# Two transformer layers on one core: q, k and v of three chunks computed with seven products for eight

## The chip, the cores and the metric

The kernel runs on one core of a Trainium2 chip. The metric is device time in microseconds (us), from the start of the program to its end. The core has a matrix engine (TensorE, PE in the profile; its weight loads are PEld), a vector engine (VectorE, DVE), a scalar engine (ScalarE, ACT), GpSimd (POOL), and SyncE (SP), which here only issues DMAs. Each engine works through its own queue in order. TensorE reads from the on-chip memory SBUF and accumulates into banks of PSUM.

## The reference

Two layers, each an attention block and an MLP block on `x` of 2048 tokens by 1024 features; both layers use the same weights.

```python
def _A_ref(x, wqkv, wo):                 # 32 heads of 32
    q, k, v = split(x @ wqkv)            # wqkv: 1024 x 3072
    # token t attends to t, t-2, ..., t-14 of its own head
    logits = einsum("bhsd,bhswd->bhsw", q, kg) * 32 ** -0.5   # masked where t-2w < 0
    o = einsum("bhsw,bhswd->bhsd", softmax(logits), vg)
    return o @ wo

def _B_ref(x, w1, w3, w2):               # w1, w3: 1024 x 3584, w2: 3584 x 1024
    return (silu(x @ w1) * (x @ w3)) @ w2

x = x + _A_ref(layernorm(x), wqkv, wo)
x = x + _B_ref(layernorm(x), w1, w3, w2)
x = x + _A_ref(layernorm(x), wqkv, wo)
x = x + _B_ref(layernorm(x), w1, w3, w2)
```

## The kernel before

**Chunks and units.** The tokens are cut into four chunks of 512 (`CH`); a unit `(l, c)` is the MLP of layer `l` on chunk `c`. The order of the program is: q, k, v of layer 0 for its four chunks (`first_q`, `q_part`), then for `u` from 0 to 7 the MLP of unit `u` (`b_stage`), and after units 1 to 4 the q, k, v of unit `u + 3`, that is of the four chunks of layer 1 (`with_q`). Attention runs in between on VectorE in halves of 256 tokens (`score_steps`, `value_steps`), its small gather and spread matmuls and the output projection (`o_tile`, L773) are put between matmuls of other work. Output projections of a chunk are done while the MLP of the chunk before it runs.

**Plain q, k, v.** `q_part` makes one of q, k, v for a chunk: for each of 8 column tiles, 8 matmuls of 128x128 by 128x512 into a PSUM bank (L831), whose stationary side is every eighth column of the weight tile (`t::KT`); ScalarE copies the bank to a stage tile (L835); two tiles at a time are stored to DRAM (`qkv_d`, L842), from where attention loads them. In layer 0 the stage tiles lie in `big`, in layer 1 in `hT`. Three parts make 192 matmuls a chunk.

**The Strassen form.** From unit 2 on (`TU`) the MLP's products use a form with 7 products for 8. `products` cuts the normalised chunk `xnT` into four quarters (two halves of features, two of 256 tokens); `norm_sums` (L288) makes three sums of quarters in `sums` and one in place; the weights come as blocks and sums of blocks that were written to DRAM earlier (`t_d`). A product is 8 matmuls of 128x128 by 128x256 (`run`, L1133). One group makes 512 output features: products P1, P5, P6, P2 use an `early` weight tile of 1 MB, P7, P3, P4 a `late` one of 768 KB. `head_part` also holds the steps between the products: ScalarE copies of accumulators (L1162, L1167, L1171), a VectorE addition (L1174), the corner on VectorE (L1186, L1189). Groups are chained: P7, P3, P4 of a group are put between P1, P5, P6 and P2 of the next. At the end of the chain `W("P1", ...)`, the first down projections, stand between the last group's tail. The down projection uses the same form (`second`, `W`, L1068).

**Sums of weights.** Units 0 and 1 run the plain form, and beside it `weight_size` squares each w1 or w3 tile on ScalarE (L871), a ones-matmul (L883) adds up, `scale_of` (L859 to L863, VectorE) makes a power-of-two scale; `weight_sums` (L901, ScalarE) casts four blocks to scaled fp16 in one of two slots in `big`, `differences` (L914, VectorE) makes three more, and two DMAs of POOL's queue write them to `t_d`. w2 is measured in layer 0's q, k, v (`part_of_w2`, L948) and summed in the down projections (L995).

**The planner.** The order of instructions is written out by the Python program, which keeps a planned clock of each engine (`now`). `pe`, `dve`, `act`, `dma` add costs to it. Work that isn't tied to a place lies in queues: `norms, makes, adds, values, scores` for VectorE (`background` takes what would end before a given time), `acts, sizes, parts, reads` for ScalarE (`act_background` takes what would end by TensorE's planned time plus 2.2 us), `pe_queue` for small matmuls. `force`, `finish_sums`, `ready_norm` emit what must be done at a point.

**Weights.** Six tiles of 1 MB (`wp`) are filled in the order of the list `seq`; `release(n)` lets n go and `flush` issues the next loads on SP's queue (L709 to L720). `held` and `release_held` keep tiles until their sums are made.

**Normalisation.** For the later chunks it runs on ScalarE (`act_norm`: L313 measures, L340 applies), and a DMA transpose on SP's queue (L342) puts it into one of two `xnT` buffers; for an MLP unit `norm_sums` follows. Side PSUM tiles (tag `sd`, two) hold projections, attention and the sums of sizes.

Of the kernel before, what the change touches and what calls it, by code (L numbers as in the profile page):

```python
# [17 lines left out]
def kernel(  # L18
# [13 lines left out]
    nc = tc.nc  # L32
# [122 lines left out]

    def bank(name):
        if name == "po":
            return side.tile([P, 512], FP32, name=name, tag="sd")
        return psum.tile([P, 512], FP32, name=name, tag="mm")
# [52 lines left out]
    up2 = const.tile([P, 1], FP32, name="up2")  # L212
    peak = const.tile([P, 3], FP32, name="peak")
    hsum = const.tile([P, HTN // 2, HT], FP16, name="hsum")
    h16 = hT[:].bitcast(FP16)
    t2_d = [dram.tile([P, 7, (b - a) // 2, 512], FP16, name=f"t2_d{i}") for i, (a, b) in enumerate(fsplits)]
    t_d = [[dram.tile([P, 14, KT // 2, P], FP16, name=f"t_d{m}_{g}") for g in range(NG)] for m in range(2)]
    qkv_d = [[dram.tile([P, KT, S], BF16, name=f"qkv_d{l}_{i}") for i in range(3)] for l in range(2)]
# [58 lines left out]
    def norm_sums(key):  # L277
# [9 lines left out]
        def step(out, x, y, op):  # L287
            return 0.62, xnT_at[key], lambda: nc.vector.tensor_tensor(out, x, y, op=op)  # L288
# [66 lines left out]

    def act_background():
        for queue in (acts, sizes, parts, reads):
            while True:
                s = head(queue)
                if s is None or max(now["act"], s[1]) + s[0] > now["pe"] + 2.2:  # L360
                    break
# [207 lines left out]
    def score_steps():  # L569

        V = nc.vector
        for g, (l, h) in enumerate(halves):
# [19 lines left out]
            def gather_heads(t):  # L592
                at["L"] = L = side.tile([P, W, BLK], FP32, name="L", tag="sd")
# [42 lines left out]
            def spread_heads(a, At=At, An=An, t2=t2, key=(l, h)):  # L636
                ps = side.tile([P, W, BLK], FP32, name="pe", tag="sd")
# [43 lines left out]
    for u in range(len(units)):  # L681
# [14 lines left out]
        if 1 <= u and u + 3 < len(units):  # L696
            seq += [("qkv", which, h) for which in range(3) for h in range(2)]
    w_tiles, w_at, due, used = [], {}, [], [0]
# [58 lines left out]
    def o_tile():  # L757
# [12 lines left out]
        for hh in range(2):  # L770
# [8 lines left out]
            dve(0.64, r)  # L779
# [12 lines left out]
    def between(hold, must=False):  # L792

        flush()
# [20 lines left out]
    def q_part(l, c, which, ws, then=()):  # L815
# [8 lines left out]
        for t0 in range(0, KT, SG):  # L824
            i = (c * 3 + which) * KT // SG + t0 // SG
            i = i % (7 if l == 0 else 8) * SG
            sgt = big[:, i * CH:(i + SG) * CH].bitcast(BF16).rearrange("p (a t) -> p a t", a=SG) if l == 0 else hT[:, i:i + SG, :]
# [16 lines left out]
            if l == 0:  # L844
                stored[:] = landed, landed
# [19 lines left out]
    def weight_size(m, g, w, at, got):  # L865
# [8 lines left out]
        def scale_item(ps, r):  # L874
            def emit():
                scale_of(ps[:], up, down)
                got["at"] = now["dve"] + 0.1
            yield 0.8, r, emit

        def add_up(t):  # L880
            ps = side.tile([P, 1], FP32, name="size", tag="sd")
            for i in range(2):
                nc.tensor.matmul(ps[:], lhsT=ones[:], rhs=size[:, m, g, i:i + 1], start=i == 0, stop=i == 1)  # L883
            makes.append([scale_item(ps, pe(2, t)), None])
# [4 lines left out]
    def weight_sums(m, g, w, got):  # L889
# [4 lines left out]
        for a in range(2):  # L894
# [9 lines left out]
            makes.append([differences(m, g, a, now["act"] + 0.1), None])  # L904
# [482 lines left out]
```

## Time and profile before

| | us |
|---|---|
| median of 3 runs | 1568.73 (1568.36 to 1570.1) |
| profiled execution | 1568.03 |
| its span | 1566.3 |
| TensorE busy / VectorE / ScalarE | 1543.1 / 1190.8 / 913.5 |
| q, k, v of layer 1 begin at | 536.5, 726.1, 917.0, 1104.9 |

The span is from the first to the last instruction; the execution holds 1.7 us around it. A line of the profile names the source line, the engine, the operation, what it writes and reads, shapes and count; then busy time, mean length of one, and the idle time just before it with what ended it. A matmul's length (379 ns for 512 columns) is its passage through the array; matmuls overlap, so their rate is read from starts.

### The profile page before, as it was taken

How to read it: one execution, taken by the hardware profiler on the slowest of the kernel's cores; microseconds unless marked ns; L12 is line 12 of the kernel's file. 1: busy time of each engine (PE TensorE's matmuls, PEld its weight loads, DVE VectorE, ACT ScalarE, POOL GpSimd, SP SyncE). 2: the span in 40 equal slices, each digit the busy share in tenths (PEclk: the TensorE clock that was granted, in tenths of full speed). 3: DMA queues.
4: the chain of work that ended last, by engine and by line, in shares of the span. 5: the costliest groups of instructions: out<-in, count | busy, mean ns of one | idle time of the engine just before them, and what ended most of it. 6: DMA issues, size and time to landing. Idle time of an engine off the chain costs nothing.

```text
span 1566.3 us, 25242 instructions
## 1 busy us (share of the span) xinstructions
PE 1543.1 (99%) x9758; PEld 999.6 (64%) x9758; DVE 1190.8 (76%) x2048; ACT 913.5 (58%) x1452; POOL 125.2 (8%) x247
## 2 busy tenths in 40 slices
PE   9999999999998999999999999999999999999999
PEld 7665544444443568585676857767677667676866
DVE  4789988988887798998779775897368977445345
ACT  4785466575755447565556754756648356544634
POOL 1111001110111100100002020000101000000000
PEclk9999999999999999999999999999999999999999
DMA  9666767898787987888869878797979977878885
GB/s 329 196 186 211 233 192 270 291 284 282 219 300 269 275 319 260 288 298 296 277 239 322 288 272 280 267 331 260 315 270 303 313 285 261 314 273 329 314 293 207
DMA packets 258360, 431.17 MB, mean 275 GB/s; under 512 B 72832, under 2 KB 200064, under 8 KB 241984
## 3 DMA queue, kind: packets, MB, share of 16 engines
q1 hardware_dynamic: 248464, 390.90, 74.9%
q0 software_dynamic: 9632, 38.54, 6.3%
q8 instruction: 76, 1.25, 0.3%
q14 instruction: 44, 0.36, 0.1%
q10 hardware_dynamic: 144, 0.13, 0.0%
HBM read 345.90 MB, written 67.90 MB: 264 GB/s over the span
## 4 chain that ended last, share of the span: by engine, by line
PE 77%; DVE 12%; DMA 6%; ACT 3%; issue 1%; SPq 0%; POOL 0%; ACTq 0%; DVEq 0%; POOLq 0%
PE st L1133 30%; PE ps L831 15%; PE w L1068 14%; PE po L773 6%; PE pg L1254 4%; PE pu L1263 4%; PE acc L1285 3%; DMA t_d<-big 2%; DVE tree L503 2%; DVE tree L583 2%; DVE tree L667 2%; DMA kT<-qkv_d 1%; DMA x_sb<-in_A_x_dram 1%; DVE st L233 1%; PE pe L638 1%
## 5 line engine op out<-in xcount | busy, mean ns | idle before, releaser
L831 PE MATMUL ps<-xnT,wqkv 128*128 128x512 f16 (+1 forms) x1472 | 322.2, 379 | 0.0
L1133 PEld LDWEIGHTS <-early 128*128 128x128 f16 x2688 | 262.7, 98 | 42.5 <-issue 2.7
L831 PEld LDWEIGHTS <-wqkv 128*128 128x128 bf16 x1472 | 210.8, 144 | 108.4 <-issue 1.7
L1068 PE MATMUL w<-t,hT 128*128 128x512 f16 x1008 | 226.3, 379 | 2.1 <-ACT big L1088 1.9
L1133 PEld LDWEIGHTS <-late 128*128 128x128 f16 x2016 | 196.8, 98 | 33.0 <-issue 3.8
L583 DVE TENSOR_TENSOR tree<-qT,kT 128x2048 bf16<-128x2048 bf16 x128 | 156.4, 1222 | 39.6 <-DMA kT<-qkv_d 22.8
L503 DVE TENSOR_TENSOR tree<-tree 128x1024 bf16<-128x1024 bf16 x256 | 175.4, 686 | 0.8
L1133 PE MATMUL st<-xnT,late 128*128 128x256 f16 x1344 | 174.2, 273 | 1.0 <-ACT big L1171 0.9
L1133 PE MATMUL st<-big,early 128*128 128x256 f16 x1344 | 172.4, 273 | 2.7 <-DVE big L288 1.3
L1068 PEld LDWEIGHTS <-hT 128*128 128x128 f16 x1008 | 98.3, 98 | 115.2 <-issue 3.4
L667 DVE TENSOR_TENSOR tree<-At,vT 128x2048 bf16<-128x2048 bf16 x128 | 156.3, 1221 | 14.2 <-ACT At L640 13.0
L1133 PE MATMUL st<-xnT,early 128*128 128x256 f16 x1344 | 166.0, 273 | 0.0
L773 PE MATMUL po<-wo,oT 128*128 128x512 bf16 x512 | 117.6, 382 | 7.3 <-DVE up_scale L859 2.9
L1162 ACT COPY st<-st 128x512 f32<-128x512 f32 x84 | 48.6, 579 | 116.7 <-PE st L1133 116.0
L1263 PE MATMUL pu<-xnT,w3t 128*128 128x512 f16 x448 | 105.8, 379 | 1.2 <-DMA w3t<-in_B_w_dram 0.7
L1254 PE MATMUL pg<-xnT,w1t 128*128 128x512 f16 x448 | 105.8, 379 | 0.0
L835 ACT CAST hT<-ps 128x512 bf16<-128x512 f32 x96 | 55.8, 586 | 82.0 <-PE ps L831 81.1
L1174 DVE TENSOR_TENSOR st<-st,big 128x512 f32<-128x512 f32 x84 | 58.5, 696 | 58.6 <-ACT big L1171 58.4
L1285 PE MATMUL acc<-w2t,hT 128*128 128x512 bf16 x448 | 98.2, 379 | 0.0
L1142 ACT ACTIVATE sg<-st,down_scale 128x512 bf16<-128x512 f32 x126 | 86.8, 689 | 12.7 <-PE st L1133 12.3
L773 PEld LDWEIGHTS <-oT 128*128 128x128 bf16 x512 | 50.5, 99 | 65.1 <-issue 10.4
L1133 PE MATMUL st<-big,late 128*128 128x256 f16 x672 | 87.1, 273 | 0.0
(171 smaller groups left out, 1946.4 us busy)
## 6 DMA issues: line engine op xcount, KB each, us to landing
early<-t_d SPq DMA_DIRECT2D x84, 1024.0 KB, 6.7
late<-t_d SPq DMA_DIRECT2D x84, 768.0 KB, 6.1
t<-t_d SPq DMA_DIRECT2D x42, 1024.0 KB, 6.6
t<-t_d SPq DMA_DIRECT2D x42, 768.0 KB, 5.1
wqkv<-in_A_wqkv_dram SPq DMA_DIRECT2D x28, 1024.0 KB, 8.5
w1t<-in_B_w_dram SPq DMA_DIRECT2D x14, 1024.0 KB, 8.0
w3t<-in_B_w_dram SPq DMA_DIRECT2D x14, 1024.0 KB, 9.2
t_d<-big POOLq DMA_DIRECT2D x28, 512.0 KB, 6.1
```

Source lines behind the costliest of these rows:

```text
L503: nc.vector.tensor_tensor(b, b, buf[:, 4:8, :], op=ALU.add)
L583: V.tensor_tensor(pr, qT[:], kT[:, :, k0:k0 + TCH], op=ALU.mult)
L667: V.tensor_tensor(tm, At[:], win, op=ALU.mult)
L773: nc.tensor.matmul(ps[:], lhsT=oT[:, t, j * P:(j + 1) * P], rhs=wo[:, t, hh * 512:(hh + 1) * 512], start=(t == 0), stop=(t == KT - 1))
L831: nc.tensor.matmul(ps[:], lhsT=ws[kk // KH][:, kk % KH, t::KT], rhs=xnT[:, kk, :], start=(kk == 0), stop=(kk == KT - 1))
L1068: nc.tensor.matmul(out[:], lhsT=lhs[:, k, j * P:(j + 1) * P], rhs=w[:, k, :], start=start and k == 0, stop=k == nq - 1, skip_group_check=True)
L1133: nc.tensor.matmul(out[:, a, :], lhsT=w[:, a, blk, k, :], rhs=rhs[:, k, :], start=start and a == 0 and k == 0, stop=k == KQ - 1, skip_grou ...
L1142: nc.scalar.activation(sg[:], src, ACTF.Silu, scale=inv)
L1174: nc.vector.tensor_tensor(G["D"][:], G["D"][:], su, op=ALU.add)
L1254: nc.tensor.matmul(pg[:], lhsT=w1t[:, kk, fi * P:(fi + 1) * P], rhs=xnT[:, kk, :], start=(kk == 0), stop=(kk == KT - 1))
L1263: nc.tensor.matmul(pu[:], lhsT=w3t[:, kk, fi * P:(fi + 1) * P], rhs=xnT[:, kk, :], start=(kk == 0), stop=(kk == KT - 1))
L1285: nc.tensor.matmul(acc[:], lhsT=hT[:, f, j * P:(j + 1) * P], rhs=tiles[hh][f // nq][:, f % nq, :], start=(f == 0), stop=(f == f1 - f0 - 1))
```

## The change

For the chunks 1, 2 and 3 of layer 1 `q_products` takes the place of `q_part`: six groups (q, k, v, each with two halves of 512 features) in the chained form, which `products` and `q_products` now share as `pipeline`. Chunk 0 of layer 1 and all of layer 0 stay plain. `t_d` gets entries 2 to 4 for wq, wk, wv, and `seq` their early and late tiles.

The sums of wqkv have one scale. ScalarE squares the six wqkv tiles in layer 0's first chunk (`size_of_qkv`). The sums for v are made from the third chunk on, in one block slot (4, in `hT`), those for q and k while chunk 0 of layer 1 runs, in slots 2, 3 and 4 (`sums_of_qkv`); for that chunk the stage tiles move to `hsum` and two rows of `hT`. Weight tiles of that chunk are let go through `held`, after their sums.

`sums`, the single buffer of token sums, is also used for the three chunks: `sum_later` is queued for them after their norm, and becomes free at the end of `q_products`.

Side tiles are now taken with `side_tile`, which first emits scale items that are open; scale items go to the head of `makes`. `act_background` has a gate of 5.0 us until the first chained stage, and 2.2 from there. Planned costs of VectorE steps and some of ScalarE are set anew. One of the differences of weights is computed from another, as an addition.

```diff
+    def side_tile(*args, **kw):
+        while opened[0]:
+            assert head(makes) is not None
+            take(makes)
+        return side.tile(*args, **kw)
...
+    room = [hT[:, 2:9, :].bitcast(FP16), hT[:, 9:16, :].bitcast(FP16)]
+    blocks += [big[:, 3072:6656].rearrange("p (b k c) -> p b k c", b=7, k=KT // 2)]
+    blocks += [r_.rearrange("p b (k c) -> p b k c", k=KT // 2) for r_ in room]
...
+    gate = [5.0]
...
-                if s is None or max(now["act"], s[1]) + s[0] > now["pe"] + 2.2:
+                if s is None or max(now["act"], s[1]) + s[0] > now["pe"] + gate[0]:
...
+        elif TU <= u and u + 3 < len(units):
+            groups = [(2 + which, g) for which in range(3) for g in range(2)]
+            for i, (m, g) in enumerate(groups):
+                seq += [("early", m, g)] + ([("late", *groups[i - 1])] if i else [])
+            seq += [("late", *groups[-1])]
...
+            if (l, c) == (1, 0):
+                i = (which * KT + t0) // SG % 3
+                sgt = (hsum_slots + [hT[:, 0:2, :]])[i]
...
-            makes.append([scale_item(ps, pe(2, t)), None])
+            makes.insert(0, [scale_item(ps, pe(2, t)), None])
...
+    def size_of_qkv(i, w):
+        ...
+            yield 1.95, 38.0, lambda: nc.scalar.activation(junk, w_[:, j * half:(j + 1) * half], ACTF.Square,
+                                                          accum_out=size_q[:, 2 * i + j:2 * i + j + 1])
...
+    def sums_of_qkv(which, ws):
+        while "at" not in got_q or norm_left.get(("Q", 0, NCH - 1), 1):
+            yield "blocked"
+        for g in range(2):
+            for a in range(2):
+                slot = 4 if which == 2 else (2, 3, 4, 2, 3, 4, 3, 4)[q_blocks[0]]
+                ...
+                    t = 4 * g + 2 * fh + a
+                    yield 0.61, max(got_q["at"], stored[slot]), lambda: nc.scalar.activation(
+                        b[:, i], ws[kh][:, :, t::KT], ACTF.Copy, scale=up_q[:])
+                makes.append([differences(2 + which, g, a, slot, now["act"] + 0.1), None])
...
+    def q_products(l, c):
+        key = ("Q", l, c)
+        ready_norm(key)
+        force(adds, lambda: key in sums_of)
+        ...
+        def consume(G, q, src, r):
+            pair, t0 = q % 2, HT * (q // 2)
+            to = stage(G, pair)
+            if q != 3:
+                nc.scalar.activation(to[:, :, t0:t0 + HT], src, ACTF.Copy, scale=down_q[:])
+            ...
+            if not G["left", pair]:
+                nc.sync.dma_start(qkv_d[l][which][:, t:t + SG, c * CH:(c + 1) * CH], to)
+        ...
+        pipeline(key, groups, consume, lambda i: between(False, i == 3))
+        sums_free[0] = True
+        xnT_free[key] = now["pe"]
...
             if f0 == 0 and i == 4 and 1 <= u and q < len(units):
                 queue_norm(("Q", *units[q]), units[q][1], range(R))
+                if u >= TU:
+                    adds.append([sum_later(("Q", *units[q])), None])
...
-        if with_q:
+        if with_q and u >= TU:
+            q_products(*units[q])
+        elif with_q:
             for which in range(3):
                 if which == 2:
                     between(False, True)
-                q_part(*units[q], which, [weight("qkv"), weight("qkv")])
-                release(2)
+                ws = [weight("qkv"), weight("qkv")]
+                if which < 2:
+                    reads.append([sums_of_qkv(which, ws), None])
+                q_part(*units[q], which, ws)
+                held.append(("q", which))
+                release_held(1)
+            finish_sums(lambda: q_blocks[0] > 6)
+            force(makes, lambda: not pending[2])
```

## The prediction

> **What bounds the kernel now.** I read the page's busy times first, then the matrix engine's timeline around one qkv stage of layer 1, the table of stretches, the groups by form and the DMA issues. Busy times, of a span of 1566.3 us:
>
> ```profile
> PE 1543.1 (99%) x9758; PEld 999.6 (64%) x9758; DVE 1190.8 (76%) x2048; ACT 913.5 (58%) x1452; POOL 125.2 (8%) x247
> ```
>
> TensorE is idle for 1566.3 - 1543.1 = 23.2 us only, so a gain must come from fewer or shorter matmuls, or from those 23 us. The timeline of TensorE (start, length, line, operation, count) shows the stage that the change rewrites, and the form that it is rewritten to:
>
> ```profile
> 917.01 41.60 PE L831 MATMUL ps<-xnT,wqkv 128*128 128x512 f16 x192
> 958.45 1.04 PE L1133 MATMUL st<-xnT,early 128*128 128x256 f16 x8
> ...
> 1001.73 1.04 PE L1133 MATMUL st<-xnT,early 128*128 128x256 f16 x8
> ...
> 1019.19 1.04 PE L1133 MATMUL st<-xnT,early 128*128 128x256 f16 x8
> ```
>
> 192 plain matmuls take 958.45 - 917.01 = 41.44 us, 215.8 ns each, without a gap. From 1001.73 to 1019.19 stand 20 products of eight matmuls: 0.873 us a product. What else runs beside the qkv stages is in the table of stretches (stretch, length, then busy us of PE, PEld, DVE, ACT, POOL, clock, DMA share, GB/s); the first row is chunk 0 of layer 1, the next two are chunks 2 and 3:
>
> ```profile
> 536.50:578.80 42.30, 42.30 (x197) 27.88 (x196) 37.10 (x64) 18.59 (x33) 0.90 (x1) 1.00 0.90 322
> 917.00:958.50 41.50, 41.50 (x194) 27.54 (x193) 20.63 (x37) 22.01 (x35) 6.20 (x10) 1.00 0.85 263
> 1105.00:1146.50 41.50, 41.50 (x195) 27.54 (x194) 10.33 (x19) 22.23 (x35) 2.95 (x9) 1.00 0.99 307
> ```
>
> The clock is full. VectorE and ScalarE have room in the later two, VectorE little in the first, and DMA little anywhere. The rows that price the added work (busy, mean ns of one):
>
> ```profile
> L831 PEld LDWEIGHTS <-wqkv 128*128 128x128 bf16 x1472 | 210.8, 144 | 108.4 <-issue 1.7
> ...
> L1133 PEld LDWEIGHTS <-late 128*128 128x128 f16 x2016 | 196.8, 98 | 33.0 <-issue 3.8
> ...
> L914 DVE TENSOR_TENSOR big<-big 128x512 f16<-128x512 f16 x112 | 47.4, 423 | 18.7 <-ACT big L901 16.3
> ...
> L901 ACT ACTIVATE big<-w3t,up_scale 128x512 f16<-128x512 bf16 x56 | 36.4, 711 | 21.8 <-DMA t_d<-big 18.2 <-DVE up_scale L863 3.5
> ...
> L871 ACT ACTIVATE hsum<-w3t 128x2048 bf16<-128x2048 bf16 x14 | 26.6, 1903 | 0.7 <-DMA w3t<-in_B_w_dram 0.6
> ...
> L288 DVE TENSOR_TENSOR big<-xnT 128x1024 f16<-128x1024 f16 x6 | 4.1, 689 | 39.4 <-DMA xnT<-xn 39.4
> ```
>
> **Part 1: the products.** A chunk's q, k, v become 6 groups of 7 products: 42 x 0.873 = 36.7 us for 41.44. That is 4.77 us a chunk, 14.3 us for three. This term is firm: the same matmul form and tile shapes already run back to back.
>
> **Part 2: the tail of each group chain.** In the MLP the last group's P7, P3, P4 are interleaved with down projections; here nothing is between them. P4 waits for VectorE's corner, which starts when P7 ends: 0.75 us (the row of L1186 has 748 ns) and two hand-overs, against 0.87 us of P3. 0 to 0.4 us, taken 0.2 each: +0.6.
>
> **Part 3: evictions.** ScalarE goes from 24 casts of 0.59 us (14.1 us) to 36 of 0.58 to 0.69 (about 23.4 us) in a stage; with the 8 us of norm work in it (22 - 14) that is 31 of 36.7 us. VectorE gets 6 x (0.70 + 0.75) = 8.7 us and 4 x 0.69 = 2.75 us for sums: 20.6 + 11.4 = 32 of 36.7. Both fit; MLP groups with norm work run at 0.86 to 1.0 of ScalarE with one 0.41 us stall (at 1067). Taken 0; up to 1 us a stage.
>
> **Part 4: one buffer of sums.** `sums` now serves the chunk's q, k, v and then the next MLP unit. Today the unit's four sums are made during the qkv stage; afterwards they wait for the stage's tail. With the corner done about 1.7 us after the tail's start, s1 is ready at 2.4 and s2 at 3.1, and the unit's P5 and P6 come at 3.5 and 4.4 us: covered, if the last transposes have landed and VectorE isn't inside a tree operation (1.2 us). The transposes land 31 us into the second and third of the stages (947.97, 1136.14), before 36.7. In the first they land 44.5 us in (770.6) and today already cost this:
>
> ```profile
> 771.46 1.92 PE L1133 MATMUL st<-big,early 128*128 128x256 f16 x16 [1.30 <-DVE big L288]
> ```
>
> The stage shrinks by 4.8 us; if the landing stays, the wait grows to about 6, if the norm work moves forward with it, it stays 1.3. Taken 3.5 there and 1 at each of the others: +4.2 against today, 0 to +8.
>
> **Part 5: sums of weights for q and k, in chunk 0 of layer 1.** 32 casts x 0.711 = 22.8 us on ScalarE's 18.6 give 41.4 of 42.3 us: full. VectorE's 32 x 0.42 = 13.5 on 37.1 is 50.6: over, but its attention has room after it (layer 0's last output projection is done at 655, and is wanted at the next stage, 726). POOL's queue writes 8 x 896 KB more, with the DMA share already 0.90. The weight tiles of q are let go one part later and those of k at the stage's end, after ScalarE has read them. So the first late tile of the next unit is issued at 579 or later, and not at 566.6, lands 6 to 8 us after, and is wanted at 586.7: 0 to 6 us of stall, taken 2. SP's queue holds v's stores and the attention loads behind that load; attention isn't late by this.
>
> The casts read every eighth element of a weight row. By the rows, reading `wqkv` with that stride costs a weight load 144 - 98 = 46 ns on 128 elements, 0.36 ns an element; a cast spends 711/512 = 1.39 ns an element. If all of it were added, a cast takes 0.18 us more, 5.8 us for 32, and ScalarE would be at 47 of 42.3 us; if the reading hides in the cast's own pace, nothing. I take the pace, and keep +5 as an end.
>
> The Trainium skill ("SBUF — State Buffer", section "Door 1: The DMA port swizzle") speaks against this part: SBUF has lines of 16 bytes and "each access that crosses to a new line pays a penalty"; eight bf16 elements are a line, so every access here does. It names no size; an estimate with the 0.833 ns an element of "ScalarE: Activation LUTs" (section "What ACT_TABLE_LOAD costs") doubled would be 0.43 us a cast, 13.7 us in the stage, and part 5 nearer to 12 than to 2.
>
> **Part 6: layer 0.** Twelve squares (1.90 + 0.19 us) are 25 us and 16 casts for v 11.4 us of ScalarE, in 40 to 199 us, where it is busy 79.7 + 25.1 of 159 us; VectorE gets 6.8 us. It fits on average. From 40 to 142 us there are only 22 free us, so ScalarE runs full and up to the new 5.0 us behind TensorE; six accumulators of 1.73 us cover 8 to 10 us of that. v has one block slot: four blocks x (2.8 cast + 1.7 difference + about 7 store) = 46 us in series from about 150 us, which ends at the stage's end. Taken +1, 0 to +4.
>
> **Part 7: the scale items.** Before unit 1's last output projections TensorE waits for a scale that VectorE reaches late:
>
> ```profile
> 488.16 0.38 PE L883 MATMUL size<-size,ones 128*128 128x1 f32 x2 [0.78 <-ACT hsum L871]
> 491.49 3.28 PE L773 MATMUL po<-wo,oT 128*128 128x512 bf16 x8 [2.94 <-DVE up_scale L859]
> 496.18 1.89 PE L773 MATMUL po<-wo,oT 128*128 128x512 bf16 x8 [1.41 <-DVE x_sb L778]
> ```
>
> The change puts scale items first in their queue and forces them before the side bank is used again. Next late is the x_sb addition (1.41). Taken -2, between -5 and 0. The planner's other figures (0.64 to 0.60 and so on) and the gate of 5.0 reorder work in the first 580 us: 0, plus or minus 2.
>
> **Part 8: weights by DMA.** A stage's weights grow from 6 MB to 6 x 1.75 = 10.5 MB. With 3 MB of stores, 1 of transposes and 1 of attention loads some 16 MB are to move in 36.7 us: 443 GB/s against 307 in the stretch whose DMA share is 0.99. The shortfall at that rate is 53 - 36.7 = 16 us. Against it: six tiles are issued before the stage begins (t2 tiles are let go every 2.6 us), an MLP tile at full pace lands 6 to 7 us after its issue and is used 12.9 us after it (8 to 7 us to spare), and behind the stage the next unit has four output projections of 3.45 us that need no weights. Walking the queue tile by tile with the packets' own durations (2.6 us for an early tile, 2.0 late, 0.75 a store, 1.75 a transpose, 2 an attention load), the least spare time I find is some 5 us, and some 2 in the third stage, whose first tiles queue with output stores. Taken +1 in all, 0 to +24.
>
> **Sum.** -14.3 + 0.6 + 0 + 4.2 + 2 + 1 - 2 + 1 = -7.5 us. On the profiled span of 1566.3 that is 1558.8; its execution took 1568.03, 1.7 us more than its span, and the median of the runs, 1568.73, is 0.7 above it: 1561.2, said as 1561.
>
> **The rivals.** (A) Full gain: transposes move forward with the stage, layer 0 hides its work and the scale waits go: -14.3 + 0.6 - 3 = about -16 to -12, 1553 to 1557. For it: VectorE and ScalarE have room in three of the four places. Against: the 44.5 us landing. (B) The gain is spent: transposes of all three stages late (+8), chunk 0 of layer 1 over by +5, layer 0 +2: 1568. For it: ScalarE at 41.4 of 42.3 us. (C) Slower: the three stages become bound by DMA. It decides when less of the shortfall is covered than leaves 14.3 / 3 = 4.8 us a stage: with 12 us short and 4 covered the stall is 8 a stage, 24 in all, less 14.3: +10, 1578. For it: the share of 0.99 in the third stage, and SP's queue, which waits for evictions before stores that stand ahead of weight loads. Against: 16 to 22 us to spare on every tile after today's stages. That the products don't replace the plain form is no case: they stand in the trace already.
>
> **How the numbers follow.** Forecast (-4 to -11) 0.50; A 0.18; B (within 3 us; 0.2%, about what a measurement of this kernel can tell, is 3.1 us) 0.13; C, or B overdone, 0.19. Faster 0.68, same 0.13, slower 0.19. The likeliest case alone is 1557 to 1565; the range that leaves out 2 in 10 reaches from the better half of A to the middle of C: 1553 to 1575.
>
> **What would show it.** TensorE's timeline in three stages: 336 matmuls of 256 columns in 36.7 us; waits of products for `early` or `late` tiles would speak for C; a wait for the sums at the start of three units (part 4) of 3.5, 1 and 1 us; a gap near 587 for part 5, with casts of wqkv at 711 ns; the 2.94 us wait gone. I am wrong if gaps inside the stages exceed 2 us each, or the casts take 0.9 us or more.

## The result, and the profile after

The changed kernel takes 1627.78 us (1626.62 to 1629.93), beside 1568.55 us for the kernel before on the same chip: a ratio of 1.0377, 95% interval 1.0359 to 1.0395. It is slower by 59 us; 1561 was predicted, with 1575 as the upper end of the range. The profiled execution's span is 1626.7 us, 60.4 more than before.

The page's busy times of the changed kernel (busy us, share of the span, instructions), and from the view by cores the span and mean granted clock of after, then of before:

```profile
PE 1554.3 (96%) x10192; PEld 1019.8 (63%) x10192; DVE 1232.9 (76%) x2149; ACT 1007.9 (62%) x1560; POOL 134.0 (8%) x271
```

```profile
core 0: 1626.7 us, clock 0.983
```

```profile
core 0: 1566.3 us, clock 0.999
```

TensorE is idle for 1626.7 - 1554.3 = 72.4 us, and was for 23.2: +49.2. The clock of TensorE is the second loss. The clock records inside the span show 11 stretches at half clock, 54.6 us together. TensorE is busy for 44.8 us of them and loses half of that, 22.4 us (the rest is idle time, counted already); before there was one stretch of 3.4 us, which cost 1.4. So +21.0. What is left is the matmul work itself: 60.4 - 49.2 - 21.0 = -9.8 us. Part 1 said -14.3 for the products. An estimate closes most of the difference: TensorE is interrupted for more than 0.1 us 49 times, and was 21 times before, and at each interruption the last matmul's passage runs out unshared (0.379 us where a matmul in a row takes 0.216, for 512 columns), 28 x 0.163 = 4.6 us. Waits and the clock, 70.2 us, took five times what the products were to save.

By stretches of the program, between the first matmuls of each, in us of the two profiled executions:

| stretch | before | after | change | predicted |
|---|---|---|---|---|
| q, k, v of layer 0 | 202.5 | 211.7 | +9.2 | +1 |
| unit 0 | 161.5 | 185.3 | +23.8 | units 0, 1: -2 |
| unit 1 | 172.6 | 175.9 | +3.3 | |
| chunk 0 of layer 1 (plain) | 42.3 | 72.0 | +29.7 | +2 |
| chunks 1 to 3 (seven products) | 125.8 | 116.7 | -9.1 | -13.7 |
| units 2 to 7 | 861.6 | 865.0 | +3.4 | +4.2 |

The table of stretches shows the places (chunk 0, then chunks 1, 2 and 3; columns as in the prediction):

```profile
572.90:644.90 72.00, 54.48 (x221) 30.29 (x220) 37.78 (x80) 51.23 (x61) 10.67 (x19) 0.86 0.79 265
790.20:829.50 39.30, 37.60 (x339) 33.03 (x338) 37.05 (x60) 31.81 (x51) 5.28 (x8) 1.00 1.01 310
975.60:1013.80 38.20, 38.20 (x350) 33.25 (x348) 26.02 (x40) 33.63 (x53) 3.10 (x9) 1.00 1.09 344
1162.50:1201.70 39.20, 37.82 (x342) 33.17 (x340) 30.72 (x51) 33.25 (x53) 4.39 (x7) 1.00 1.06 333
```

The middle stage is busy for all of its 38.20 us: no product waits, with a DMA share of 1.09. TensorE's timeline answers the lines of 917 to 1019 shown before:

```profile
975.66 1.04 PE L1105 MATMUL st<-xnT,early 128*128 128x256 f16 x8
976.54 1.91 PE L1105 MATMUL st<-big,early 128*128 128x256 f16 x16
978.28 1.91 PE L1105 MATMUL st<-xnT,early 128*128 128x256 f16 x16
...
1013.86 1.04 PE L1105 MATMUL st<-xnT,early 128*128 128x256 f16 x8
1017.15 1.15 PE L1105 MATMUL st<-big,early 128*128 128x256 f16 x5 [2.26 <-DVE big L305]
```

Chunk 0 is where half of the loss lies: of its 29.7 us, 17.5 are idle time of TensorE and 7.1 are lost to the clock; the rest goes with 24 more small matmuls than before (x221 for x197). The groups of ScalarE (line, output <- input, shapes, count | busy, mean ns | idle before), among them the casts with stride (L979) and the contiguous ones of w1 (L932):

```profile
L979 ACT ACTIVATE hT<-wqkv,up_q 128x512 f16<-128x512 bf16 x40 | 47.2, 1241 | 6.2 <-DMA t_d<-hT 6.1
L932 ACT ACTIVATE big<-w1t,up_scale 128x512 f16<-128x512 bf16 x56 | 36.2, 713 | 9.9 <-DVE up_scale L892 5.1 <-DVE tree L686 3.5 <-DMA t_d<-big 1.3
L959 ACT ACTIVATE hsum<-wqkv 128x2048 bf16<-128x2048 bf16 x12 | 24.3, 2025 | 0.0
L979 ACT ACTIVATE big<-wqkv,up_q 128x512 f16<-128x512 bf16 x8 | 9.4, 1229 | 9.4 <-DMA t_d<-big 9.4
```

A cast that reads every eighth column takes 1.24 us, not 0.71. ScalarE's timeline in chunk 0 shows what else holds it, and TensorE's what follows:

```profile
575.31 1.24 ACT L979 ACTIVATE big<-wqkv,up_q 128x512 f16<-128x512 bf16 x1
585.94 3.45 ACT L979 ACTIVATE big<-wqkv,up_q 128x512 f16<-128x512 bf16 x3 [9.39 <-DMA t_d<-big]
589.29 3.38 ACT L979 ACTIVATE hT<-wqkv,up_q 128x512 f16<-128x512 bf16 x3
592.58 0.56 ACT L864 CAST hsum<-ps 128x512 bf16<-128x512 f32 x1
...
618.89 0.58 ACT L864 CAST hsum<-ps 128x512 bf16<-128x512 f32 x1 [1.79 <-DMA qkv_d<-hsum]
625.56 1.19 ACT L979 ACTIVATE hT<-wqkv,up_q 128x512 f16<-128x512 bf16 x1 [6.08 <-DMA t_d<-hT]
626.66 0.57 ACT L864 CAST hsum<-ps 128x512 bf16<-128x512 f32 x1
```

```profile
593.20 5.70 PE L860 MATMUL ps<-xnT,wqkv 128*128 128x512 f16 x16 [4.60 <-ACT hsum L864]
...
627.28 3.57 PE L860 MATMUL ps<-xnT,wqkv 128*128 128x512 f16 x8 [5.06 <-ACT hsum L864]
...
640.97 0.86 PE L657 MATMUL pe<-E,spread 128*128 128x512 bf16 x2 [3.09 <-ACT At L659]
```

The block slot of the first sums of q, slot 2, lies where the w2 blocks of unit 1 still wait for their store: the second cast stands for 9.39 us. The engine works in order, so every eviction of q behind it stands too (592.58), TensorE runs out of free accumulators, and stops for 4.60 us. The same again at 625.56, where a slot is used a second time before its store has landed. Then the clock: stretches after two of TensorE's gaps (588.6 to 593.2, and 1014.9 to 1017.2), with the granted clock as the number behind the five engines:

```profile
580.00:588.60 8.60, 8.60 (x40) 5.59 (x39) 0.00 (x0) 2.66 (x3) 0.00 (x0) 1.00 0.85 329
590.60:597.40 6.80, 4.20 (x10) 1.63 (x10) 5.16 (x13) 6.80 (x8) 1.09 (x2) 0.50 0.44 174
1017.20:1020.60 3.40, 3.40 (x17) 2.46 (x18) 3.37 (x5) 0.60 (x1) 0.00 (x0) 0.51 1.12 368
```

All 11 stretches at half clock begin within or right after a gap, or a cluster of gaps, that holds one of more than 2 us; each lasts 3.4 or 6.8 us.

In layer 0 and unit 0 the waits of TensorE end with ScalarE again, but for the last, a tile of w3 (TensorE's timeline, then ScalarE's):

```profile
137.44 0.60 PE L1047 MATMUL size<-size_q,ones 128*128 128x12 f32 x2 [5.71 <-ACT At L659]
...
211.46 0.40 PE L1047 MATMUL size<-size,ones 128*128 128x16 f32 x2 [4.72 <-ACT At L659]
...
320.47 3.11 PE L1378 MATMUL pg<-xnT,w1t 128*128 128x512 f16 x8 [3.82 <-ACT sg L1382]
...
332.76 3.60 PE L1387 MATMUL pu<-xnT,w3t 128*128 128x512 f16 x8 [5.26 <-DMA w3t<-in_B_w_dram]
```

```profile
131.42 1.91 ACT L1012 ACTIVATE hsum<-hT 128x2048 bf16<-128x2048 bf16 x1 [2.99 <-DMA hT<-in_B_w_dram]
...
314.94 5.01 ACT L1063 ACTIVATE big<-w2t,up 128x512 f16<-128x512 bf16 x8 [7.52 <-DMA t_d<-big]
319.85 1.53 ACT L1382 ACTIVATE sg<-pg 128x512 bf16<-128x512 f32 x3
```

The longest wait of all, 5.71 us, is new work of layer 0: the matmul that adds up the new squares stands in TensorE's queue until casts of attention are done, and ScalarE has got to them late, behind squares of w2 that waited 2.99 us for their tile. At 314.94 eight casts of w2 that exist before too come ahead of three silus; they wait 7.52 us for a slot's store, and the silus with them. In unit 0 nothing of wqkv is made: the order is another. Why, the experiments had to tell.

### The profile page after: what moved, and what is told of

The parts are those of the page before. It is cut to its first block, busy times and chain, and to the rows that moved or that the text cites. A ratio compares the mean times of both kernels' runs of the same rounds, so it can differ in the third digit from the quotient of the medians.

```text
span 1626.7 us, 26521 instructions
## 1 busy us (share of the span) xinstructions
PE 1554.3 (96%) x10192; PEld 1019.8 (63%) x10192; DVE 1232.9 (76%) x2149; ACT 1007.9 (62%) x1560; POOL 134.0 (8%) x271
## 4 chain that ended last, share of the span: by engine, by line
PE 46%; DVE 9%; ACT 4%; DMA 3%; issue 1%; POOL 0%; ACTq 0%; DVEq 0%; POOLq 0%
PE st L1105 31%; PE w L1254 11%; PE po L797 4%; DVE tree L686 1%; DMA xnT<-xn 1%; DVE tree L522 1%; DVE x_sb L1239 1%; ACT hT L979 1%; DVE tree L602 1%; DVE hT L1325 1%; DVE hT L1225 1%; DMA kT<-qkv_d 1%; DMA t_d<-big 1%; DVE big L305 1%; DMA t_d<-hT 0%
## 5 line engine op out<-in xcount | busy, mean ns | idle before, releaser
L1105 PEld LDWEIGHTS <-early 128*128 128x128 f16 x3264 | 320.1, 98 | 52.8 <-issue 4.4
L1105 PEld LDWEIGHTS <-late 128*128 128x128 f16 x2448 | 239.1, 98 | 42.3 <-issue 8.0
L860 PE MATMUL ps<-xnT,wqkv 128*128 128x512 f16 (+1 forms) x896 | 206.7, 391 | 11.6 <-ACT hsum L864 11.6
L1105 PE MATMUL st<-big,early 128*128 128x256 f16 x1632 | 210.8, 274 | 5.2 <-DVE big L305 2.3
L1105 PE MATMUL st<-xnT,late 128*128 128x256 f16 x1632 | 211.5, 273 | 3.3 <-DVE big L1143 1.9
L1105 PE MATMUL st<-xnT,early 128*128 128x256 f16 x1632 | 201.2, 273 | 0.0
L860 PEld LDWEIGHTS <-wqkv 128*128 128x128 bf16 x896 | 129.3, 145 | 86.9 <-issue 25.7
L1129 DVE TENSOR_TENSOR st<-st,big 128x512 f32<-128x512 f32 x102 | 70.8, 694 | 65.0 <-ACT big L1126 64.8
L1105 PE MATMUL st<-big,late 128*128 128x256 f16 x816 | 105.8, 273 | 1.6 <-DVE st L1129 1.5
L1387 PEld LDWEIGHTS <-w3t 128*128 128x128 bf16 x448 | 44.4, 99 | 61.0 <-DMA w3t<-in_B_w_dram 6.7
```

The lines of the kernel that those rows point to most:

```text
L860: nc.tensor.matmul(ps[:], lhsT=ws[kk // KH][:, kk % KH, t::KT], rhs=xnT[:, kk, :], start=(kk == 0), stop=(kk == KT - 1))
L1105: nc.tensor.matmul(out[:, a, :], lhsT=w[:, a, blk, k, :], rhs=rhs[:, k, :], start=start and a == 0 and k == 0, stop=k == KQ - 1, skip_grou ...
L1129: nc.vector.tensor_tensor(G["D"][:], G["D"][:], su, op=ALU.add)
L1387: nc.tensor.matmul(pu[:], lhsT=w3t[:, kk, fi * P:(fi + 1) * P], rhs=xnT[:, kk, :], start=(kk == 0), stop=(kk == KT - 1))
```

## The experiments

Times are medians, ratios are to runs of the kernel before on the same chip, with the 95% interval. Theory 1: the loss is the work and the waits of the weight sums. Theory 2: it is the gate of 5.0 us, and the new planned costs, which reorder work. Theory 3 (the prediction's rival C): products wait for weight tiles.

**The two halves.** `e1_products` has the products without the sums (its weight blocks are w1's, of the same shapes, so q, k and v of three chunks are not the real ones) and the narrow gate; `e2_sums` has the sums without the products.

```diff
# e1_products
-            v = t_d[i][n][:, 0:8] if early else t_d[i][n][:, 8:14]
+            src = t_d[i][n] if i < 2 else t_d[0][2 * (i - 2) + n]
+            v = src[:, 0:8] if early else src[:, 8:14]
-    gate = [5.0]
+    gate = [2.2]
-                if which < 2:
-                    reads.append([sums_of_qkv(which, ws), None])
...
# e2_sums
-            q_products(*units[q])
+            for which in range(3):
...
+                q_part(*units[q], which, [weight("qkv"), weight("qkv")])
+                release(2)
```

> The seven-product form alone: no squares of wqkv and no casts for its sums (the three stages read blocks that were made from w1, so q, k, v of these chunks are wrong), stage tiles of chunk 0 in hT as before, gate 2.2 throughout. Theory 1 (the loss is ScalarE's work for the sums of weights: squares, and casts of 1.24 us) and theory 2 (the loss is the gate, which lets ScalarE run 5.0 us behind): both expect 1555 to 1563, the three stages with their units 562 us as in the changed kernel, or a little less. Theory 3 (the products themselves cost it, by DMA or by waits in the chain): 1568 or more.

Measured: 1577.07 us, 1.0057 [1.0040, 1.0075]. The total is in theory 3's range; the places, below, speak against it.

> The sums of weights alone: squares, casts, differences, stores and the gate as in the changed kernel, but q, k, v of all four chunks of layer 1 plain. Theories 1 and 2: as slow as the changed kernel or slower by what the products save, 1628 to 1640, chunk 0 of layer 1 at 70 us again. Theory 3: 1568 to 1590.

Measured: 1625.82 us, 1.0368 [1.0352, 1.0383]. That is just under the lower end of theories 1 and 2: the sums half alone has nearly all of the loss. The products' three stages are 38.2, 39.9 and 37.8 us in e1_products, against 43.0, 41.4 and 41.4; that its total is still above before comes from units 0 and 1, 168 and 181 us against 162 and 173, where only the planned costs and the handling of scale items differ. Theory 3 falls: no more than 0.4 us of any wait there is for an early or late tile, and the one wait at the start of a following unit is Part 4's:

```profile
781.23 1.04 PE L1107 MATMUL st<-big,early 128*128 128x256 f16 x4 [2.38 <-DVE big L306]
```

**The gate.** `e3_gate22` is the changed kernel with the gate of before.

```diff
-    gate = [5.0]
+    gate = [2.2]
```

> The changed kernel with one number changed, the gate 2.2 instead of 5.0 us from the start. Theory 2: most of the 27 us of units 0 and 1 and of the 9 us of layer 0 go, 1585 to 1600. Theory 1: the same work meets the same forced points, 1615 to 1640. Theory 3: 1628.

Measured: 1692.92 us, 1.0798 [1.0776, 1.0821]: 65 us worse, in neither theory's range. With the added work, a narrow gate lets less of it be done beside TensorE; what is left is forced at the deadlines. In one place TensorE waits 23.0 us for a silu (227 to 250 us): on ScalarE the sixteen casts for v stand ahead of it, with three waits of 4.8 to 5.1 us for their one slot. So in the kernel as changed the narrow gate is no remedy; theory 2 as stated had the sign wrong there.

**The planned costs.** `e5_costs` is the kernel before with the new costs and nothing else; three runs take single figures of it, and `e9_products_old` is e1_products with the old ones.

```diff
# e15_diffcost, and the same at L1001
-            yield 0.46, r, lambda: nc.vector.tensor_tensor(b[:, out], b[:, x], b[:, y], op=ALU.subtract)
+            yield 0.36, r, lambda: nc.vector.tensor_tensor(b[:, out], b[:, x], b[:, y], op=ALU.subtract)
# e17_silucost
-                    ts = act(0.5, r, "silu")
+                    ts = act(0.58, r, "silu")
# e18_prodcost, and the same at L779 and L1297
-                    th = dve(0.64, r)
+                    th = dve(0.60, r)
# e5_costs: all of these, and
-                G["tD"] = dve(0.68, max(t, G["t5"])) + 0.1
+                G["tD"] = dve(0.61, max(t, G["t5"])) + 0.1
...
```

> The kernel before with the changed kernel's planned costs of VectorE and ScalarE steps alone (0.46 to 0.36 for a difference of weights, 0.64 to 0.60, 0.69 to 0.66, 0.68 to 0.61 and so on); no work is added or taken. Run e1 lost 15 us in units 0 and 1, where it has no new work. If the new planned costs do that (theory 4: casts are planned to follow stores that have not landed, and block ScalarE's queue), this is 1580 to 1587, with the loss in the second half of unit 0 and in unit 1. If it is the handling of scale items and held tiles: 1566 to 1572.

Measured: 1583.99 us, 1.0099 [1.0083, 1.0115].

> As e1 (the seven-product form alone, no squares and casts for wqkv; blocks of w1 in place of wqkv's, so q, k, v of three chunks are wrong), but with the planned costs of the kernel before. If the costs took e1's 15 us and the products bring what e1's three stages showed: 1560 to 1566, units 0 and 1 as before, the three stages with their units 562 to 564 us for 566. If the products bring the 14.3 us that were predicted: 1552 to 1557. If the products lose by themselves: 1568 or more.

Measured: 1558.44 us, 0.9936 [0.9912, 0.9961]. That is between the two values expected: with the old costs the products make the kernel 10 us faster than before, where Parts 1, 2 and 4 add up to 9.5. The new costs take that and more. They change no instruction, only the order.

> The kernel before with one planned cost changed, the difference of weight sums from 0.46 to 0.36 us, in the two places that have it. If e5_costs' 15.2 us come from this figure (VectorE gets more side work planned into units 0 and 1 than it can do, since the trace has 0.42), 1580 to 1586. If they come from the other figures (silu 0.50 to 0.58, products 0.64 to 0.60), 1566 to 1572.

Measured: 1564.03 us, 0.9974 [0.9956, 0.9992]: a little faster, so this figure alone is not it.

> The kernel before with one planned cost changed: the silu of units 0 and 1 from 0.50 to 0.58 us (the line whose wait, 9.4 us in e5_costs, holds TensorE). If this figure alone moves the order of ScalarE's casts against the silu, 1578 to 1586 as in e5_costs; if the 15 us need the other figures, 1564 to 1570.

Measured: 1650.34 us, 1.0516 [1.0498, 1.0535]. Neither value expected: one figure, moved towards what the profile measures (0.60 us), costs 82 us.

> The kernel before with one planned cost changed: VectorE's product of units 0 and 1 and its additions after plain projections from 0.64 to 0.60 us. If this figure alone moves the order, 1578 to 1586; if the 15 us need the silu's figure or several together, 1564 to 1570.

Measured: 1584.02 us, 1.0097 [1.0081, 1.0113]. The effects don't add: one figure +82, one +16, one -5, all together +15. In e17_silucost 66 of the 84 us of span are in chunk 0 of layer 1, by the mechanism seen above (ScalarE's timeline, then TensorE's):

```profile
562.09 5.01 ACT L995 ACTIVATE big<-w2t,up 128x512 f16<-128x512 bf16 x8 [12.97 <-DMA t_d<-big]
571.44 2.56 ACT L995 ACTIVATE big<-w2t,up 128x512 f16<-128x512 bf16 x4 [4.33 <-DMA t_d<-big]
573.90 2.99 ACT L835 CAST hT<-ps 128x512 bf16<-128x512 f32 x6
```

```profile
574.52 19.16 PE L831 MATMUL ps<-xnT,wqkv 128*128 128x512 f16 x80 [8.87 <-ACT hT L835]
...
619.89 1.04 PE L596 MATMUL L<-psm,gather 128*32 128x512 bf16 x8 [17.49 <-DVE psm L507]
```

Casts of w2 got in front of the evictions and wait for slots; attention, set behind, then has TensorE wait for VectorE, 17.49 us at once. So it is not that a figure is wrong by itself: as these traces read, the order of before happens to keep such casts out of the evictions' way, and small shifts undo that.

**Which sums, and the gate without work.** Two by two: `e13_sums_v` is e2_sums with layer 0's squares and sums for v only, `e14_sums_qk` with chunk 0's sums for q and k only, `e16_products_gate5` is e1_products (no sums of wqkv) with the gate of 5.0.

```diff
# e13_sums_v
-                if which < 2:
-                    reads.append([sums_of_qkv(which, ws), None])
-                held.append(("q", which))
-                release_held(1)
+                release(2)
# e14_sums_qk
-                for i in range(6):
-                    parts.append([size_of_qkv(i, w_tiles[i]), None])
-                reads.append([sums_of_qkv(2, w_tiles[4:6]), None])
# e16_products_gate5
-    gate = [2.2]
+    gate = [5.0]
```

> The kernel of e2_sums without the sums for q and k in chunk 0 of layer 1: squares, scale, the sums for v in layer 0, the gate of 5.0 and the new planned costs stay; the weight tiles of chunk 0 are let go as before the change; q, k and v are plain in all chunks. If the loss of the sums sits where the stage table shows it, in the stages in which the work is done, the stage of chunk 0 returns from 69.7 to 42 us and the rest stays as in e2_sums: 1625.8 - 28 = about 1598. If the late units 0 and 1 are the consequence of chunk 0's weight tiles being held, they return too: 1584 to 1590, which is e5_costs and little more.

Measured: 1605.76 us, 1.0233 [1.0215, 1.0251], above both values expected.

> The kernel of e2_sums without the squares and without the sums for v in layer 0: the scale of wqkv is a constant 1, chunk 0 of layer 1 makes the sums for q and k as in the changed kernel. If the loss is additive by place, layer 0 returns to 201 us and the start of unit 0 to 90, and chunk 0 costs its 28: e5_costs' 1584 + 28 = about 1612. If chunk 0's stage was late only since layer 0's work pushed ScalarE back, it shrinks to 45 to 50: 1585 to 1592.

Measured: 1626.88 us, 1.0374 [1.0355, 1.0393], far above both: the sums of q and k alone are as slow as all of them.

> The kernel of e1_products with the gate of 5.0 us in place of 2.2: seven products for eight alone, on blocks of w1's sums, no squares and no sums for wqkv. If a wider gate by itself lets ScalarE's side work delay what TensorE waits for in units 0 and 1, 1582 to 1600 against 1577 of e1_products. If it matters only together with the added work, 1574 to 1580.

Measured: 1597.63 us, 1.0180 [1.0156, 1.0203], as expected of a gate that delays by itself. The time until unit 2 begins, where all the sums are done, from the profiled executions (us):

| kernel | layer 0 | units 0, 1 | chunk 0 | until unit 2 |
|---|---|---|---|---|
| before | 202.5 | 334.1 | 42.3 | 578.8 |
| products, old costs, gate 2.2 (e9) | 202.0 | 336.5 | 44.1 | 582.6 |
| new costs, gate 2.2 (e1) | 202.3 | 348.7 | 42.5 | 593.5 |
| new costs, gate 5.0 (e16) | 195.1 | 366.6 | 49.9 | 611.6 |
| the same and layer 0's sums (e13) | 208.9 | 360.0 | 46.5 | 615.4 |
| the same and chunk 0's sums (e14) | 194.8 | 367.7 | 74.8 | 637.3 |
| both (e2) | 210.6 | 360.6 | 70.3 | 641.6 |
| as changed | 211.7 | 361.2 | 72.0 | 644.9 |

At this point the parts do add. Layer 0's sums: 615.4 - 611.6 = 3.8 without the others, 641.6 - 637.3 = 4.3 with them. Chunk 0's sums: 25.7 and 26.2; this includes what the change does for them, stage tiles in `hsum` and weight tiles held longer, which no run separates. The new costs and the gate of 5.0, with none of the work: 29.0 (10.9 for the costs, 18.1 more with the gate). What else the change emits differently costs 3.8 (e9 less before). So of the 66.1 us that the changed kernel is late here, some 33 are order, 26 the sums of q and k, 4 those of layer 0; the last 3 stay unassigned, and each row is one execution. A part of theory 2 stands after all: the gate alone costs 20 us where there is no added work, and is worth 65 where there is. The waits in e16_products_gate5 are the silu's and, behind it, w3's:

```profile
PE pg L1379 <- ACT sg L1383: 16.1, 3, 11.1
PE pu L1388 <- DMA w3t<-in_B_w_dram: 10.7, 2, 6.8
```

(us in all, times, longest). The silu behind the 11.1 us stood behind two runs of w2's casts, which waited 2.29 and 4.08 us for stores.

**What the q and k sums cost.** `e4_contig` casts 128 neighbouring columns in place of every eighth (q, k, v then come from permuted blocks); `e12_contig_slots` also uses the slots as 3, 4, 2 and has the row order to match; `e7_paired` makes one instruction of two casts, which reads pairs and writes with a stride; `e8_paired_slots` has both.

```diff
# e4_contig
-                        b[:, i], ws[kh][:, :, t::KT], ACTF.Copy, scale=up_q[:])
+                        b[:, i], ws[kh][:, :, t * P:(t + 1) * P], ACTF.Copy, scale=up_q[:])
# e12_contig_slots (and e8_paired_slots), on top
-                slot = 4 if which == 2 else (2, 3, 4, 2, 3, 4, 3, 4)[q_blocks[0]]
+                slot = 4 if which == 2 else (3, 4, 2, 3, 4, 2, 3, 4)[q_blocks[0]]
# e7_paired
+                    yield 1.06, max(got_q["at"], stored[slot]), lambda: nc.scalar.activation(
+                        b[:, i0:i1:kh + 1].rearrange("p f k c -> p k c f"),
+                        ws[kh][:].rearrange("p k (c t) -> p k c t", t=KT)[:, :, :, t:t + 3:2], ACTF.Copy, scale=up_q[:])
```

> The changed kernel with the 48 casts of wqkv reading 128 neighbouring columns instead of every eighth (the blocks then belong to other columns, so q, k, v of three chunks are wrong). Theory 1 in its sharp form (the stride makes 0.71 us 1.24): casts of 0.71 us, chunk 0 of layer 1 from 72 to 45 to 55 us, 1600 to 1613. If ScalarE's waits for stores of earlier blocks (9.4 and 6.1 us) are the cause there, the stage stays above 60 us and the time above 1617. Theories 2 and 3: 1620 or more.

Measured: 1615.18 us, 1.0301 [1.0285, 1.0317]. The cast falls from 1242 to 722 ns (min, median, max):

```profile
L979 ACT ACTIVATE hT<-wqkv,up_q x40: 706/722/761, 144.4 to 625.2; 128x512 f16<-128x512 bf16 x40
```

The time lies just above the range of the sharp form of theory 1, and chunk 0 above its 45 to 55: the stride is worth 12.6 us, 10.0 of them in chunk 0 (72.0 to 62.0), and ScalarE's waits for slots stay (9.48 us the longest).

> As e10 with the changed kernel's own planned costs: e4 with the slot order 3, 4, 2 (and the stores that put the order right). If ScalarE's wait for the last w2 blocks (9.5 us in e4) is a cause by itself, chunk 0 of layer 1 goes from 61 to 50 to 54 us and the time to 1604 to 1610; if another wait takes its place, 1612 to 1618.

Measured: 1611.08 us, 1.0274 [1.0250, 1.0298]. Chunk 0 is 53.8 us now, as expected if the wait is a cause by itself, and the time lies between the two ranges: unit 2 is 152.6 for 145.3, with 6.0 us of gaps, and of 8 us won by the slots' order 4 arrive.

> The changed kernel with each pair of casts of wqkv as one instruction that reads two elements of every group of eight (24 casts of 1024 for 48 of 512, the same blocks). If a cast's time goes by the lines touched (theory 1), one takes some 1.3 us and chunk 0 of layer 1 needs 20 us less of ScalarE: 1608 to 1618, near e4's 1615. If by elements read apart, 2.3 us and no gain: 1625 to 1630.

Measured: 1689.04 us, 1.0760 [1.0737, 1.0783].

> As e7, and the first block of chunk 0 of layer 1 in slot 3 in place of slot 2 (order 3, 4, 2, 3, 4, 2, 3, 4), which lies over the two slots that the last w2 blocks are still being stored from. If that wait of ScalarE (9.4 us) is what the stage still loses with short casts, the stage goes from about 60 to 45 to 50 us and the time to 1595 to 1606; if another wait takes its place, it stays within 5 us of e7.

Measured: 1681.12 us, 1.0725 [1.0700, 1.0750]. Both miss: the paired cast takes 4.96 us for the two of 1.24. The values that it writes are not those of the two casts, for a reason that no run shows, so these two runs price this form of instruction and nothing else.

```profile
L979 ACT ACTIVATE hT<-wqkv,up_q 128x1024 f16<-128x1024 bf16 x20 | 96.6, 4964 | 5.2 <-DMA t_d<-hT 5.2
```

**The scale items, and a repair.** `e6_firsts` is the kernel before with Part 7's edit (scale items first, side tiles after them). `e10_repaired` has e12's casts and slots with the old costs, `e11_repaired_sample` moreover two squares for twelve.

```diff
# e6_firsts
-            makes.append([scale_item(ps, pe(2, t)), None])
+            makes.insert(0, [scale_item(ps, pe(2, t)), None])
# e11_repaired_sample
-                for i in range(6):
-                    parts.append([size_of_qkv(i, w_tiles[i]), None])
+                parts.append([size_of_qkv(0, w_tiles[0]), None])
```

> The kernel before with the changed kernel's handling of scale items alone: at the head of their queue, forced before a side tile is taken, and held tiles let go at every step between column tiles. Theory 4: 1563 to 1570, the wait of 2.9 us at 488 gone. If this handling costs units 0 and 1 their 15 us: 1580 to 1587.

Measured: 1567.42 us, 0.9995 [0.9986, 1.0004]: no difference. The wait of 2.94 us at 488 is gone, and others have come: 2.25 us for a scale at 386, 4.76 for a tile of w2 at 446.

> The changed kernel with three parts altered: casts of wqkv from 128 neighbouring columns (the order of q, k, v is put right by the store to DRAM), first block of chunk 0 in slot 3 and not 2, planned costs of the kernel before. Gate 5.0 as in the changed kernel. By adding parts (e4: -12.6; costs: -15; slot: -5 to -9) 1587 to 1600. If the costs and the new work's stalls are the same time counted twice: 1600 to 1612.

Measured: 1635.50 us, 1.0423 [1.0377, 1.0469]. Both ranges expected are missed: the old costs, worth 19 us to e1_products, lose 24 here (against e12). Its costliest wait is for the token sums, at unit 2 (9.8 us, the longest) and twice behind it, and output projections wait for attention:

```profile
PE st L1105 <- DVE big L305: 17.7, 3, 9.8
PE po L797 <- DVE oT L526: 11.1, 7, 2.4
```

> As e10, with two squares in place of twelve (the scale of wqkv is taken from one tile). If the 25 us of squares are what fills ScalarE in layer 0, that stage goes from about 207 to 201 to 203 us and the time 4 to 8 us under e10; if the casts for v and the gate do it, less than 3 us.

Measured: 1615.75 us, 1.0302 [1.0279, 1.0325]: ten squares fewer (2.3 us of ScalarE each) are worth 20 us here, where 4 to 8 were expected, though layer 0's sums as a whole cost 4 in the table above. In the profiled executions layer 0 itself isn't shorter (209.5 us for 207.4); units 0 and 1, chunk 0 and what follows are: here too the order is another.

No version with the sums in it beat the kernel before. e9_products_old does, but on borrowed blocks; of those with the whole computation only e15_diffcost is faster, by 0.3% and with one planned figure changed.

## Why the prediction was wrong

**Part 1, the products: right.** A product takes the 0.87 us that it was priced at (976.54 to 978.28 is two). The three stages shrank by 9.1, not 13.7: small attention matmuls that were elsewhere now lie in them, and TensorE idles for 3.1 us there. **Part 2 and 3: right.** No wait inside the stages exceeds 1.3 us; at most 0.9 of ScalarE is used.

**Part 4, one buffer of sums: wrong in place, and near in size by luck.** +4.2 was predicted for waits of 3.5, 1 and 1 against the 1.30 of before. What came is one wait of 2.26 at unit 4 in the changed kernel (in e1_products one of 2.38, at unit 3), with 3.4 us of half clock behind it, which no term held; units 2 to 7 are +3.4.

**Part 5, the sums for q and k: the first step that failed.** Taken +2, measured 26 by the start of unit 2 (e14 less e16, e2 less e13). Three terms show in the traces; what each is worth apart from the others is measured for the first two alone. The cast was priced at 0.711 with +5 us as an end for the stride, from the 46 ns that a strided weight load adds; the row was of another engine, and ScalarE adds 0.53 us a cast, 17 us of its time for 32, past the 0.9 us that the prediction had named as a sign of being wrong. Removing it from all 48 casts gives 12.6 us. The rule that I set aside was the better guide: the Trainium skill, "SBUF — State Buffer", section "Door 1: The DMA port swizzle", says that an access that crosses to a new line pays; the prediction's estimate by it was 0.43 a cast, and the measurement is 0.53. The doubling in that estimate was a guess, and no run tries another stride, so that new lines are the reason isn't shown. Second, the prediction asked when weight tiles are let go, and not when a block slot comes free: slot 2 shares room with w2's blocks, and a cast that waits for a store has all evictions behind it (9.39 and 6.08 us). Another order of the slots takes 8 us off the stage (e12 against e4). The prediction had asked who stands behind a waiting instruction of SP's queue (rival C), not of ScalarE's. Third, the half clock after the gaps: 20 us at half in this stage, 7.1 us lost.

**Part 6, layer 0: right in sign, small.** Taken +1 with 0 to +4; 3.8 to 4.3 by the start of unit 2. In layer 0 itself the sums cost 13.8 (208.9 less 195.1); units 0 and 1 and chunk 0 are 10 shorter for it.

**Part 7, "0, plus or minus 2" for the planned figures and the gate: the second step that failed.** They cost 29 us by unit 2 (e16 less e9) and 39 by the end, and units 0 and 1 show it. I had read them as bookkeeping; in a program whose order is emitted from planned clocks they are the change. The trace of before shows how near the order stands to the edge: there too casts wait for stores (`L901`, 21.8 us idle, 18.2 on t_d), without TensorE noticing. The -2 for the scale items is nothing (e6): the 2.94 us wait is gone, and others took its place.

**Part 8 and rival C: right to take little.** DMA share of 1.0 to 1.09 in the stages and no stall on tiles. Rival B, "the gain is spent", had the right place (chunk 0 over) at a fifth of the size. No rival held the mechanism that the traces show in unit 0 and chunk 0: ScalarE's queue blocked by a wait for a slot, TensorE stopped, and its clock halved.

**The clock** was in no term of the sum. The trace of before has one gap cluster followed by 3.4 us at half clock (488 to 495), and I did not price it. The Trainium skill, "TensorE: Matmul & The Clock Gate", section "What's actually happening", gives half rate after at least one idle window of some 3.4 us; here a gap of 2.26 us, alone, was followed by 3.4 us at 0.5, and the measurement decides. As a rule of thumb from this kernel, idle time costs some 40% more by the clock: 49 us more of it came with 21 us more lost.

What stays open: why the silu's planned cost alone does more than all the figures together, and why the parts that add up by unit 2 don't in e10 and e11. The runs show where the time goes, not which decision of the planner turns first.

## What to carry to other kernels

On an engine that works in order, a wait for a store is paid by everything queued behind it: before adding producers with few buffers to the engine that also evicts accumulators, list each buffer's earlier user and when its store lands. Where the program's order is generated from planned costs, an edit of a cost is an edit of the schedule, worth tens of microseconds in either sign, and has to be tried by itself. Price an access pattern by a row of the same engine, and allow for the clock behind stalls of TensorE of 2 us and more.

## What the runs showed of the hardware

ScalarE reads 512 bf16 elements spaced by 16 bytes in 1.23 to 1.24 us, against 0.71 for neighbours; with fp16 writes scattered as well, 1024 elements take 4.96 us, four strided casts' time for the work of two. A weight load on TensorE pays less for the same stride: 145 against 98 ns. In the changed kernel TensorE's clock fell to half for 3.4 or 6.8 us at each of the 11 gaps of 2.1 to 5.7 us, and gaps under 2 us standing alone left it full. The length alone doesn't decide it: in e12_contig_slots a gap of 3.69 us left the clock full, and in e2_sums one of 1.99 us was followed by 3.4 us at half, which one of the same length at the same place of the changed kernel was not.
